# Score masks copied by VectorE, token sums and tail in halves: a recurrent memory-attention step on one core

## The chip, the cores and the metric

The kernel runs on one core of a Trainium2 chip. The metric is the device time of one execution in microseconds (us). Five engines of the core work side by side, each on its own list of instructions: TensorE (PE in the profile, its weight loads PEld), VectorE (DVE), ScalarE (ACT), GpSimd (POOL) and SyncE (SP, which issues DMAs). PE writes its results into eight banks of the accumulator memory PSUM, which DVE and ACT read and write too.

## The reference

The output mixes two branches per token with a gate. Branch B is a two-layer MLP over all 2048 tokens. Branch A goes through the tokens in 64 segments of 32 and carries a memory of 8 rows from one segment to the next:

```python
g = _sigmoid((x * gate_w).sum(-1, keepdims=True))
idx = jnp.arange(L)                                   # L = 8 + 32
mask = (idx[:, None] < M) | (idx[:, None] >= idx[None, :])
mem = mem0
for s in range(n_seg):                                # 64 segments
    xs = x[:, s * seg_len:(s + 1) * seg_len, :]
    h = jnp.concatenate([mem, xs], axis=1)
    q, k, v = h @ Wq, h @ Wk, h @ Wv                  # 32 heads of 128
    scores = jnp.where(mask, q @ k.T * scale, -1e9)
    o = (softmax(scores) @ v) @ Wo
    mem = o[:, :M]                                    # the next step's memory
    outs.append(o[:, M:])
return g * concat(outs) + (1 - g) * B(x)
```

(The lines are shortened.) A step needs the memory rows that the step before has made.

## The kernel before, in words

First all weights are loaded and branch B is computed, with the product (1 - g) * b stored for later. Then come the 64 steps, and a tail. The order of every instruction on every engine is the order of the code: the part from the MLP to the end stands under `tc.manual_schedule()`, and waits are put in where one engine's result is used by another.

**Rows of a step.** Four segments make one tile T of 128 tokens; a step is `s`, with `T, si = divmod(s, 4)`. The step's input `hT` has 32 columns: 24 of the segment's tokens and the 8 memory rows. The other 8 tokens of each of the four segments do not need the memory for their q, k and v; they are projected a tile ahead, for all four segments together. This work, and the output projection of those left tokens a tile later, is the *side work* (`side`, `left_qk`, `left_v`, `wo_left`): a generator per step of 8 units of four matmuls of 512 columns. `run(n)` issues n of them at the place where it stands. `WS` gives for each `si` the numbers W1, W2 and W3 that `run` gets at three places of the step. The last tile has no next one to project, so its first two steps have no side work.

**One step** on PE, in order:

- q and k of the 32 columns, in four groups of 16 matmuls (`qk_unit`, line 120), for two halves of the heads into banks U0 to U3. Each is cast by ACT to `Tb` (line 125) and turned by a DVE transpose into `QT` or `KT` (line 129).
- `scores(s, 0)`: the scores of heads 0 to 15 into bank SbF, 16 matmuls of line 257 and four of line 261. Before them the mask stands in the bank already, and the scores are added to it. One ACT instruction takes the exponential into `E` (line 706).
- four `v_unit`s of the first value half (line 139) into X1.
- `mask_mm(1)` (line 249): four matmuls of 224 columns that put the mask `Mk`, times the identity, into bank W.
- one unit of the second value half into X2, then `msum(0)` (lines 268 and 271): the exponentials' sums for the 8 memory queries, which DVE turns into reciprocals (line 702) and multiplies into E (line 703). These two are `mnorm`.
- `scores(s, 1)` into bank W, and two exponentials of it (line 695), the memory queries' first.
- two more units of the second value half, `msum(1)` and `mnorm(1)`, the last unit. ACT casts the two value halves to `V` (lines 710 and 724).
- W1 units of side work; `xsums` (line 614): 16 matmuls of four columns, the sums for the token queries, into 8 columns of bank SbF. `recip_x` takes their reciprocals on DVE (line 625), sends them through DRAM to all partitions (`Rb`), copies the memory reciprocals (line 631) and adds them to `racc` on POOL. The token rows are normalised with `Rb` only in the next step, on POOL (line 640).
- `av` (lines 281 and 286): probabilities times values, first heads 0 to 15, then 16 to 31, into U0 to U3. ACT casts the memory rows to `UT` (line 732), then the token rows to `XR`.
- W2 units; the output projection `wo_pass` (line 151), 32 matmuls into bank W, cast in two halves to `w` (line 647).
- `mask_mm(0)` for the next step into SbF; W3 units; for the first step of a tile `out_sel`, which puts a finished tile's output together; then `new_mem` (line 654), which turns the 8 memory rows of w into columns. DVE casts them into the next step's `hT` (line 656), on which the next q and k wait.

**Last step and tail.** Step 63 needs no new memory. The sums of its tokens go into SbF (`sums`), DVE takes a reciprocal of 256 columns (line 760) and multiplies it into E, while PE runs `out_sel` for the last tile but one and the projection of step 62. Then come `av`, `wo_left` (eight units), the projection of step 63, and the last tile's output: five selecting matmuls into X2 (lines 786 and 788), one DVE instruction (line 791) and one DMA. Beside it runs a check: DVE reduces `rmin` and `racc` (lines 777 and 778) to `good`, one matmul (line 783) counts the good partitions, and a branch that is not taken here would repeat the branch in a safe form.

Of the kernel before, what the change touches and what calls it, by code (L numbers as in the profile page):

```python
# [27 lines left out]
def kernel(ctx, tc, A_x, A_mem0, A_Wq, A_Wk, A_Wv, A_Wo, A_seg_len, B_x, B_w1, B_b1, B_w2, B_b2, gate_w, out):  # L28
# [46 lines left out]
    Mk = ep.tile([P, 4, EW], BF16)  # L75
# [171 lines left out]
    def mask_mm(i2):  # L247
        for j in range(4):
            nc.tensor.matmul(Sb[i2][32 * j:32 * j + 32], lhsT=ident[:, 32 * j:32 * j + 32], rhs=Mk[:],  # L249
                             start=True, stop=True, skip_group_check=True, tile_position=(0, 32 * j))  # L250
# [41 lines left out]
    with tc.tile_pool(name="mlpw", bufs=1) as mlpw, \  # L292
# [70 lines left out]
        nc.gpsimd.memset(Mk[:], 0.0)  # L363
# [212 lines left out]
    mask_mm(0)  # L576
# [29 lines left out]
    xs8 = SbF[:, 256:256 + NG]  # L606
    RW = 9 * NG

    def xsums(s, E):

        for first, c0, n in ((True, 8, 32), (False, 0, LEFT)):
            for i in range(NG):
                c, h = i % 4, i // 4
                nc.tensor.matmul(xs8[32 * c:32 * c + n, 4 * h:4 * h + 4], lhsT=E[:, i, c0:c0 + n], rhs=BO[:, 0:P:32],  # L614
                                 start=first and h == 0, stop=not first, skip_group_check=True, tile_position=(0, 32 * c))
# [7 lines left out]
    def recip_x(s):  # L623
        R = Rs.pop(s)
        nc.vector.reciprocal(out=R[:, 8 * NG:RW], in_=xs8)

        Rb = cw.tile([P, P, NG], FP32, tag="Rb", bufs=1, name="Rb")
        nc.sync.dma_start(r_dr[s % 2][:], R[:, 8 * NG:RW])
        nc.sync.dma_start(Rb[:].rearrange("p r e -> p (r e)"), r_dr[s % 2][:].rearrange("r e -> (r e)").partition_broadcast(P))
        for i2 in (1, 0):  # L630
            nc.vector.tensor_copy(out=R[:, 32 * i2:32 * i2 + 32], in_=RP[i2])
        nc.gpsimd.tensor_tensor(out=racc[:, 0:RW], in0=racc[:, 0:RW], in1=R[:, 0:RW], op=ALU.add)  # L632
        Rbs[s] = Rb
# [25 lines left out]
    WS = ((3, 2, 0), (2, 2, 2), (2, 2, 2), (2, 2, 2))  # L659
    for s in range(nseg):  # L660
# [18 lines left out]
        for n, (t, hf) in enumerate(((0, 0), (1, 0), (0, 1), (1, 1))):  # L679
# [6 lines left out]
            qk_tr(qk_cast(bk[:]), (QT, KT)[t], hf, LEFT * (1 - t))  # L686
        V = cw.tile([P, NG, Dh], BF16, tag="V", name="V")
# [21 lines left out]
        mask_mm(1)  # L709
        nc.scalar.copy(out=v_out(V, 0), in_=X1[:])  # L710
        v_unit(X2, hc, 1, 0)
        if not last:
            msum(0)
            mnorm(0)
# [3 lines left out]
        for kc in range(1, 3):  # L718
            v_unit(X2, hc, 1, kc)
        if not last:  # L720
            msum(1)
            mnorm(1)
        v_unit(X2, hc, 1, 3)
        nc.scalar.copy(out=v_out(V, 1), in_=X2[:])  # L724
        if last:
            break
        run(W1)
        xsums(s, E)
# [10 lines left out]
        mask_mm(0)  # L739
# [17 lines left out]
    for _ in out_sel(T - 1, X2):  # L757
        pass
    nc.gpsimd.memset(UL[T % 2][:, :, :, LEFT * si:seg], 0.0)
# [10 lines left out]
    for _ in wo_left(T, X1):  # L770
# [3 lines left out]
    nc.gpsimd.tensor_tensor(out=racc[:, nx], in0=racc[:, nx], in1=R[:, nx], op=ALU.add)  # L774
# [7 lines left out]
    wf = wo_pass(UF)  # L782
    nc.tensor.matmul(X1[0:1, 0:1], lhsT=good[:, 0:1], rhs=good[:, 1:2], start=True, stop=True)
    bad = okp.tile([1, 1], I32)
    nc.vector.tensor_scalar(out=bad[:], in0=X1[0:1, 0:1], scalar1=-1.0, scalar2=float(P), op0=ALU.mult, op1=ALU.add)
    nc.tensor.matmul(X2[:], lhsT=SelL[:], rhs=wls.pop(T)[:], start=True, stop=False, skip_group_check=True)
    for i in range(SPT):
        nc.tensor.matmul(X2[32 * i:32 * i + 32, :], lhsT=(SelR if i < si else SelI)[:], rhs=(ws.pop(SPT * T + i) if i < si else wf)[:],
                         start=False, stop=True, skip_group_check=True, tile_position=(0, 32 * i))
    o = cw.tile([P, Dm], BF16, tag="o", name="o")  # L790
    nc.vector.scalar_tensor_tensor(out=o[:], in0=X2[:], scalar=g_all[:, T:T + 1], in1=cs.pop(T)[:], op0=ALU.mult, op1=ALU.add)
    nc.sync.dma_start(out2[T * P:(T + 1) * P, :], o[:])
# [123 lines left out]
```

## Time and profile before

| | us |
|---|---|
| median of 3 runs | 777.28 |
| runs | 776.89 to 779.0 |
| profiled execution | 779.11 |
| its span, first to last instruction | 777.3 |
| granted TensorE clock, share | 0.997 |
| MLP and loads (until the first step) | 0 to 95.97 |
| steps 0 to 62 | 95.97 to 757.14 |
| step 63 and tail | 757.14 to 777.3 |

How its rows are read. A row of the groups has line, engine, operation, output<-inputs, shape, count, then busy time in us, mean ns of one instruction, and the engine's idle time before them with what ended it. A row of the timeline has start in us, length, engine, line, operation, output<-inputs, count of merged instructions, and in brackets the idle time before it and the releaser. A row of the chain has start, length in the chain, engine, output and line, count. A row of the table by stretches has the stretch, its length, and for PE, PEld, DVE, ACT and POOL the busy time and the number of instructions in it, then the clock and the DMA share and rate. Matmuls on different 32-column parts of the array overlap, so a group's mean length is not what one of them costs.

### The profile page before, as it was taken

The numbers are of one execution on the slowest core, as the hardware profiler recorded it, in microseconds if no ns is written. First come the engines' busy times: TensorE is split into PE (matmuls) and PEld (weight loads), VectorE is DVE, ScalarE is ACT, GpSimd is POOL, SyncE is SP. The second block draws the span as 40 slices with busy tenths as digits, with TensorE's granted clock in tenths as the row PEclk, the third lists the DMA queues.
The fourth block names the chain that finished last, engine by engine and source line by source line (L and its number), as shares of the span: only waits on it lengthen the run. The fifth ranks groups of instructions, "written<-read, shape, count | busy, mean of one in ns | idle before, by whom it ended". The sixth has DMA issues, their size and how long they took to land.

```text
span 777.3 us, 44300 instructions
## 1 busy us (share of the span) xinstructions
PE 759.5 (98%) x19673; PEld 419.6 (54%) x19687; DVE 345.4 (44%) x1235; ACT 529.6 (68%) x1439; POOL 278.6 (36%) x523
## 2 busy tenths in 40 slices
PE   7999999999999999999999999999999999999996
PEld 5666555555555555555555555555555555555453
DVE  5776344434334343434444444435343434444334
ACT  4666676677767677667777777677776777676663
POOL 4111034333344433344434333443334344343342
PEclk9999999999999999999999999999999999999999
DMA  6779421222121222212132312212222212122221
GB/s 194 276 248 387 137 58 62 75 61 90 62 71 54 77 72 74 77 57 74 51 88 61 89 62 79 67 56 72 78 72 65 83 36 88 61 81 62 70 61 44
DMA packets 53174, 70.61 MB, mean 91 GB/s; under 512 B 21289, under 2 KB 42898, under 8 KB 51442
## 3 DMA queue, kind: packets, MB, share of 16 engines
q1 hardware_dynamic: 51250, 64.84, 26.4%
q8 instruction: 156, 2.56, 1.4%
q0 software_dynamic: 784, 1.97, 0.7%
q10 hardware_dynamic: 944, 0.92, 0.4%
q14 instruction: 40, 0.33, 0.1%
HBM read 56.96 MB, written 4.45 MB: 79 GB/s over the span
## 4 chain that ended last, share of the span: by engine, by line
PE 96%; DVE 2%; issue 1%; DMA 1%; ACT 0%; POOL 0%; DVEq 0%; ACTq 0%; POOLq 0%
PE U L120 29%; PE X L139 18%; PE W L151 15%; PE X L120 7%; PE U L466 4%; PE X L151 4%; PE U L281 3%; PE SbF L460 2%; PE W L460 2%; PE U L654 2%; PE U L268 1%; PE W L257 1%; PE SbF L257 1%; PE W L249 1%; PE SbF L614 1%
## 5 line engine op out<-in xcount | busy, mean ns | idle before, releaser
L640 POOL TENSOR_TENSOR UT<-XR,Rb 128x384 bf16<-128x384 bf16 x126 | 140.2, 1134 | 305.8 <-DMA Rb<-r_dr 226.2
L125 ACT CAST Tb<-U 128x512 bf16<-128x512 f32 x258 | 151.0, 585 | 76.4 <-PE U L120 75.9
L120 PEld LDWEIGHTS <-hT 128*32 128x32 bf16 x4096 | 104.5, 96 | 109.4 <-DVE hT L656 16.2
L139 PE MATMUL X<-Wv_sb,hT 128*32 128x512 bf16 x2048 | 151.4, 379 | 0.0
L120 PE MATMUL U<-Wq_sb,hT 128*32 128x512 bf16 x2048 | 133.3, 380 | 0.5 <-DVE hT L656 0.2
L120 PE MATMUL U<-Wk_sb,hT 128*32 128x512 bf16 x2048 | 132.6, 379 | 0.0
L151 PE MATMUL W<-Wo_sb,UT 128*32 128x512 bf16 x2080 | 125.7, 380 | 1.9 <-ACT UT L732 1.2
L656 DVE CAST hT<-U 128x16 bf16<-128x16 f32 x126 | 21.9, 175 | 207.6 <-PE U L654 199.9
L129 DVE STREAM_TRANSPOSE QT<-Tb 128x256 f32<-128x256 f32 x128 | 57.0, 446 | 80.3 <-ACT Tb L125 80.2
L151 PEld LDWEIGHTS <-UT 128*32 128x32 bf16 x2080 | 58.6, 96 | 57.7 <-issue 17.4
L620 ACT CAST XR<-U 128x256 bf16<-128x256 f32 x252 | 78.6, 439 | 0.0
L129 DVE STREAM_TRANSPOSE KT<-Tb 128x256 f32<-128x256 f32 x128 | 57.0, 446 | 46.8 <-ACT Tb L125 46.8
L647 ACT CAST w<-W 128x256 bf16<-128x256 f32 (+1 forms) x128 | 41.9, 378 | 49.0 <-PE W L151 49.0
L640 POOL TENSOR_TENSOR UL<-XR,Rb 128x128 bf16<-128x128 bf16 x126 | 60.2, 500 | 0.0
L139 PEld LDWEIGHTS <-hT 128*32 128x32 bf16 x2048 | 49.0, 94 | 20.7 <-issue 0.2
L632 POOL TENSOR_TENSOR racc<-racc,R 128x72 f32<-128x72 f32 x63 | 21.2, 337 | 99.1 <-PE U L286 69.9
L732 ACT CAST UT<-U 128x64 bf16<-128x64 f32 x252 | 35.3, 227 | 28.2 <-PE U L286 28.2
L724 ACT CAST V<-X 128x512 bf16<-128x512 f32 x64 | 37.4, 585 | 22.5 <-PE X L139 22.5
L466 PE MATMUL U<-w_sb,hTm 128*128 128x512 bf16 (+1 forms) x163 | 49.5, 381 | 0.6
L460 PEld LDWEIGHTS <-w_sb 128*128 128x128 bf16 (+1 forms) x352 | 34.6, 102 | 19.5 <-issue 1.3
L710 ACT CAST V<-X 128x512 bf16<-128x512 f32 x64 | 37.5, 585 | 9.4 <-PE X L139 1.1
L125 ACT CAST Tb<-X 128x512 bf16<-128x512 f32 x62 | 36.9, 595 | 8.0 <-PE X L120 6.2
(158 smaller groups left out, 1169.9 us busy)
## 6 DMA issues: line engine op xcount, KB each, us to landing
Rb<-r_dr SPq DMA_DIRECT2D x63, 512.0 KB, 4.0
Wv_sb<-in_A_Wv_dram SPq DMA_DIRECT2D x4, 1024.0 KB, 6.4
Wq_sb<-in_A_Wq_dram SPq DMA_DIRECT2D x4, 1024.0 KB, 7.1
Wk_sb<-in_A_Wk_dram SPq DMA_DIRECT2D x4, 1024.0 KB, 9.6
Wo_sb<-in_A_Wo_dram SPq DMA_DIRECT2D x4, 1024.0 KB, 15.3
VP<-VL SPq DMA_DIRECT2D x64, 64.0 KB, 3.3
c<-c_dr SPq DMA_DIRECT2D x16, 128.0 KB, 2.9
out_dram<-o SPq DMA_DIRECT2D x16, 128.0 KB, 1.9
```

Source lines behind the costliest of these rows:

```text
L120: nc.tensor.matmul(bk[32 * j:32 * j + 32, :], lhsT=G[:, kc, :], rhs=W5[t][:, kc, h0:h1, j, :], start=(kc == 0), stop=(kc == KC - 1), tile_ ...
L125: nc.scalar.copy(out=Tb[:], in_=bk.rearrange("p (a b e) -> p a e b", a=8, b=2))
L129: nc.vector.transpose(out=dst[:, 8 * hf:8 * hf + 8, c0:c0 + 32, :].rearrange("p a r b -> p a (r b)").bitcast(FP32), in_=Tb[:].rearrange("p ...
L139: nc.tensor.matmul(bk[32 * j:32 * j + 32, :], lhsT=G[:, kc, :], rhs=Wv5[:, kc, 4 * vb:4 * vb + 4, j, :], start=(kc == 0), stop=(kc == KC - ...
L151: nc.tensor.matmul(bk[32 * c:32 * c + 32, :], lhsT=U_[:, j, i, :], rhs=Wo_sb[:, 4 * i + j, :], start=(n == 0), stop=(n == NW - 1), tile_po ...
L460: nc.tensor.matmul(hp[:rows, 0:TB * P], lhsT=w1_sb[:, kc, fc * P:fc * P + rows], rhs=yTs[blk][:, kc, :], start=(kc == 0), stop=(kc == KC - 1))
L466: nc.tensor.matmul(bp(blk, tt)[:], lhsT=hTm[blk % 2][:rows, fc, tt * P:(tt + 1) * P], rhs=w2_sb[:rows, fc, :], start=(fc == 0), stop=(fc = ...
L620: nc.scalar.copy(out=XR[:, j], in_=U[j][:, 0:NG * 40].rearrange("p (i q) -> p i q", q=40)[:, :, 0:32])
L640: nc.gpsimd.tensor_tensor(out=out[:, :, 4 * h:4 * h + 4, o:o + b - a], in0=XR[:, :, 4 * h:4 * h + 4, a:b], in1=Rb[:, h, :, :, a:b], op=ALU ...
L647: nc.scalar.copy(out=w[:, a:a + Dm // parts], in_=W[:, a:a + Dm // parts])
L710: nc.scalar.copy(out=v_out(V, 0), in_=X1[:])
L724: nc.scalar.copy(out=v_out(V, 1), in_=X2[:])
```

## The change

- The mask is no longer made by PE. `mask_put(i2)` is one DVE copy from `MkF` into the bank. For bank W it stands after the first transpose of the step; for bank SbF it stands at the end of `recip_x`, for the next step, and covers 8 further columns with zeros, where the token sums are then added.
- `xsums` is cut in two: the eight matmuls of heads 0 to 15 stand ahead of `msum(0)`, the other eight where all stood.
- `msum(1)` and `mnorm(1)` stand behind the last value unit, and not ahead of it. The cast of the second value half is issued ahead of them in the code.
- `WS` moves one unit of side work from ahead of the projection to behind it, in the steps with si of 1, 2 and 3.
- Tail: `out_sel` writes bank X1; three of the eight `wo_left` units stand ahead of step 62's projection; racc's last sum goes from POOL to DVE; the last projection is cast in halves; the selecting matmuls that do not need it stand ahead of the check's matmul and write two banks by halves of the columns; the last matmul, the DVE instruction and the output DMA come in two halves each.

```diff
-    Mk = ep.tile([P, 4, EW], BF16)
+    MkF = ep.tile([P, 4 * EW + NG], BF16)
+    Mk = MkF[:, 0:4 * EW].rearrange("p (a c) -> p a c", c=EW)
...
-    def mask_mm(i2):
-        for j in range(4):
-            nc.tensor.matmul(Sb[i2][32 * j:32 * j + 32], lhsT=ident[:, 32 * j:32 * j + 32], rhs=Mk[:],
-                             start=True, stop=True, skip_group_check=True, tile_position=(0, 32 * j))
+    def mask_put(i2):
+        c = 4 * EW + (NG if i2 == 0 else 0)
+        nc.vector.tensor_copy(out=(SbF, W)[i2][:, 0:c], in_=MkF[:, 0:c])
...
-    xs8 = SbF[:, 256:256 + NG]
+    xs8 = SbF[:, 4 * EW:4 * EW + NG]
...
-    def xsums(s, E):
-
-        for first, c0, n in ((True, 8, 32), (False, 0, LEFT)):
-            for i in range(NG):
-                c, h = i % 4, i // 4
-                nc.tensor.matmul(xs8[32 * c:32 * c + n, 4 * h:4 * h + 4], lhsT=E[:, i, c0:c0 + n], rhs=BO[:, 0:P:32],
-                                 start=first and h == 0, stop=not first, skip_group_check=True, tile_position=(0, 32 * c))
+    def xsums(E, h):
+
+        for c0, n in ((8, 32), (0, LEFT)):
+            for c in range(4):
+                nc.tensor.matmul(xs8[32 * c:32 * c + n, 4 * h:4 * h + 4], lhsT=E[:, 4 * h + c, c0:c0 + n], rhs=BO[:, 0:P:32],
+                                 start=False, stop=True, skip_group_check=True, tile_position=(0, 32 * c))
...
             nc.vector.tensor_copy(out=R[:, 32 * i2:32 * i2 + 32], in_=RP[i2])
+        mask_put(0)
...
-    WS = ((3, 2, 0), (2, 2, 2), (2, 2, 2), (2, 2, 2))
+    WS = ((3, 2, 0), (2, 1, 3), (2, 1, 3), (2, 1, 3))
...
             qk_tr(qk_cast(bk[:]), (QT, KT)[t], hf, LEFT * (1 - t))
+            if n == 0:
+                mask_put(1)
...
-        mask_mm(1)
         nc.scalar.copy(out=v_out(V, 0), in_=X1[:])
         v_unit(X2, hc, 1, 0)
         if not last:
+            xsums(E, 0)
             msum(0)
             mnorm(0)
...
-        for kc in range(1, 3):
+        for kc in range(1, KC):
             v_unit(X2, hc, 1, kc)
-        if not last:
-            msum(1)
-            mnorm(1)
-        v_unit(X2, hc, 1, 3)
         nc.scalar.copy(out=v_out(V, 1), in_=X2[:])
         if last:
             break
+        msum(1)
+        mnorm(1)
         run(W1)
-        xsums(s, E)
+        xsums(E, 1)
...
-        mask_mm(0)
         run(W3)
...
-    for _ in out_sel(T - 1, X2):
+    nc.gpsimd.memset(UL[T % 2][:, :, :, LEFT * si:seg], 0.0)
+    for _ in out_sel(T - 1, X1):
         pass
-    nc.gpsimd.memset(UL[T % 2][:, :, :, LEFT * si:seg], 0.0)
+    fill = wo_left(T, X2)
+    run(3)
...
-    for _ in wo_left(T, X1):
+    for _ in fill:
         pass
...
-    nc.gpsimd.tensor_tensor(out=racc[:, nx], in0=racc[:, nx], in1=R[:, nx], op=ALU.add)
+    nc.vector.tensor_tensor(out=racc[:, nx], in0=racc[:, nx], in1=R[:, nx], op=ALU.add)
...
-    wf = wo_pass(UF)
-    nc.tensor.matmul(X1[0:1, 0:1], lhsT=good[:, 0:1], rhs=good[:, 1:2], start=True, stop=True)
+    wf = wo_pass(UF, 2)
+
+    wl, c = wls.pop(T), cs.pop(T)
+    halves = ((X1, slice(0, Dm // 2)), (X2, slice(Dm // 2, Dm)))
+    for bk, cc in halves:
+        for i in range(SPT):
+            nc.tensor.matmul(bk[32 * i:32 * i + 32, cc], lhsT=SelL[:, 32 * i:32 * i + 32], rhs=wl[:, cc], start=True, stop=False,
+                             skip_group_check=True, tile_position=(0, 32 * i))
+        for i in range(si):
+            nc.tensor.matmul(bk[32 * i:32 * i + 32, cc], lhsT=SelR[:], rhs=ws[SPT * T + i][:, cc], start=False, stop=True,
+                             skip_group_check=True, tile_position=(0, 32 * i))
+    nc.tensor.matmul(U[0][0:1, 0:1], lhsT=good[:, 0:1], rhs=good[:, 1:2], start=True, stop=True)
...
-    nc.vector.scalar_tensor_tensor(out=o[:], in0=X2[:], scalar=g_all[:, T:T + 1], in1=cs.pop(T)[:], op0=ALU.mult, op1=ALU.add)
-    nc.sync.dma_start(out2[T * P:(T + 1) * P, :], o[:])
+    for bk, cc in halves:
+        nc.tensor.matmul(bk[32 * si:32 * si + 32, cc], lhsT=SelI[:], rhs=wf[:, cc], start=False, stop=True,
+                         skip_group_check=True, tile_position=(0, 32 * si))
+        nc.vector.scalar_tensor_tensor(out=o[:, cc], in0=bk[:, cc], scalar=g_all[:, T:T + 1], in1=c[:, cc], op0=ALU.mult, op1=ALU.add)
+        nc.sync.dma_start(out2[T * P:(T + 1) * P, cc], o[:, cc])
```

10 lines of the change are left out of this document (3 added, 7 removed).

## The prediction

> **What bounds the kernel now.** I read the page's engine totals first, then the groups of the lines that go, the chain that ended last, a table of single memory steps, and the timeline inside three of them.
>
> ```profile
> span 777.3 us, 44300 instructions
> PE 759.5 (98%) x19673; PEld 419.6 (54%) x19687; DVE 345.4 (44%) x1235; ACT 529.6 (68%) x1439; POOL 278.6 (36%) x523
> ```
> ```profile
> L249 PE MATMUL SbF<-Mk,ident 128*32 128x224 bf16 x256 | 19.2, 259 | 0.0
> L249 PE MATMUL W<-Mk,ident 128*32 128x224 bf16 x256 | 17.5, 259 | 0.0
> ```
> ```profile
> 405.46 0.10 PE W L249 x4
> ...
> 407.22 0.10 PE SbF L614 x15
> ...
> 410.11 0.10 PE SbF L249 x4
> ```
>
> Matmuls overlap, so the chain's shares count: each group of four mask matmuls holds 0.10 us of it, two per step. On this reading PE is the bound and the 128 groups are worth 12.8 us. The table of single steps says otherwise: a first step of a tile, a later step with side work, and a step of the last tile, which has no side work.
>
> ```profile
> 348.50:359.17 10.67, 10.67 (x308) 5.76 (x308) 3.94 (x16) 7.70 (x22) 4.05 (x7) 1.00 0.26 63
> 411.16:421.49 10.33, 10.33 (x300) 5.54 (x297) 4.82 (x17) 7.21 (x21) 4.07 (x7) 1.00 0.14 40
> 736.47:746.80 10.33, 9.24 (x264) 4.94 (x264) 4.38 (x15) 6.49 (x19) 4.02 (x7) 1.00 0.27 78
> ```
>
> The third has 36 matmuls fewer and PE idle for 1.09 us, and lasts as long as the second. So 48 of the 63 steps (10.33 us) are set by the round trip from the memory rows back to themselves; only the 15 first steps of tiles (10.67 us) have PE work on it. In the step without side work the waits name the round trip's links:
>
> ```profile
> 742.50 0.58 ACT L724 CAST V<-X 128x512 bf16<-128x512 f32 x1 [0.35 <-PE X L139]
> 743.14 0.17 PEld L281 LDWEIGHTS <-V 32*128 32x128 bf16 x16 [0.17 <-ACT V L724]
> 743.86 1.91 PE L151 MATMUL W<-Wo_sb,UT 128*32 128x512 bf16 x32 [0.41 <-ACT UT L732]
> 746.24 0.49 PE L654 MATMUL U<-SelM,w 128*32 128x8 bf16 x16 [0.38 <-ACT w L647]
> ```
>
> The second half of av waits for the second value cast, the projection for UT, the new memory for w. From the step's start these stand at 6.67, 7.39 and 9.77 us. The step with side work has them at the same places:
>
> ```profile
> 415.46 0.45 DVE L129 STREAM_TRANSPOSE KT<-Tb 128x256 f32<-128x256 f32 x1 [0.37 <-ACT Tb L125]
> 415.96 0.18 PEld L257 LDWEIGHTS <-KT 128*32 128x32 bf16 x16
> 416.12 0.63 PE L139 MATMUL X<-Wv_sb,hT 128*32 128x512 bf16 x8
> 416.41 0.42 ACT L695 ACTIVATE E<-W 128x64 bf16<-128x64 f32 x2
> 416.68 0.20 PE L268 MATMUL U<-E,BO 128*32 128x32 bf16 x4
> 417.03 0.37 DVE L702 RECIPROCAL W<-U 128x32 f32<-128x32 f32 x1
> 417.18 0.58 ACT L724 CAST V<-X 128x512 bf16<-128x512 f32 x1 [0.35 <-PE X L139]
> 417.44 0.22 DVE L703 TENSOR_TENSOR E<-E,W 128x64 bf16<-128x64 bf16 x1
> 417.82 0.27 PE L281 MATMUL U<-E,V 32*128 32x40 bf16 x16
> 418.54 1.91 PE L151 MATMUL W<-Wo_sb,UT 128*32 128x512 bf16 x32
> 420.92 0.21 PE L654 MATMUL U<-SelM,w 128*32 128x8 bf16 x8
> ```
>
> (Its start is 411.16: 6.66, 7.38, 9.76.) The Trainium skill, "Perfetto Trace Analysis", section "Identifying the Most-Contended Engine", says that matmul busy time is no good measure, and to take weight-load busy time. By that, 98% is not the bound and 54% leaves room; the equal steps agree.
>
> **The change, part by part.**
>
> *Mask for bank W.* Four matmuls (0.10 us) leave the place ahead of the second scores, and eight token-sum matmuls come in, half of line 614's 0.10: PE arrives 0.05 us earlier. But KT is transposed by 415.46 + 0.45 = 415.91 and its load begins 0.05 later, at 415.96. That stays. Worth 0.
>
> *The second memory sums* move behind the last value unit. Today they start at 416.68, just after the first exponential (416.41 + 0.21, half of the row's 0.42, + 0.06). Three units at 0.21 from 416.12 end at 416.76: 0.08 later. From the sums to the reciprocal is 0.35 and to the end of line 703 another 0.63, so E is ready at 417.74 and av's second half goes on 0.05 later, at 417.79, against 417.82. The value cast is no longer last: its last unit starts at 416.55 (416.12 and two units), no longer behind the sums of 416.68 with their 0.05 of issue, so the cast's 417.18 + 0.58 = 417.76 becomes 417.57. What is late next is therefore the DVE pair. Gain 0.03 us in each of 48 steps, 1.4 us; the ends are 0.19 (were the cast alone to set it, at 417.63) and -0.1 (the sums 0.13 later than I reckon). I take 0.03, since every link of the DVE pair is read from the row of the same instruction. Queued behind the waiting av are the rest of av, UT, the projection and the next step.
>
> *The same in the first steps*, with three side units between sums and av:
>
> ```profile
> 354.02 0.20 PE L268 MATMUL U<-E,BO 128*32 128x32 bf16 x4
> ...
> 354.94 0.27 PE L614 MATMUL SbF<-BO,E 128*32 128x4 bf16 x16
> ...
> 355.28 0.28 PE L281 MATMUL U<-E,V 32*128 32x40 bf16 x16
> ```
>
> Here 1.26 us of PE work runs from sums to second av. A value unit (0.21) and half the token sums (0.05) leave it: 1.00. Started 0.08 later, av's second half comes at 355.10; by the DVE pair (354.10 + 0.35 + 0.63 + 0.05) at 355.13. Gain 0.15 us in 15 steps, 2.2 us.
>
> *Mask for bank SbF and the side units (WS).* Its 0.10 us and two units lay between projection and new memory, where even an empty PE waits for w (746.24, above). One unit comes over from ahead of the projection: 1.71 + 0.64 = 2.35 us, inside the 2.38 from 418.54 to 420.92. Ahead of the projection the empty PE waits for UT as well, so the unit's departure gives nothing. Worth 0 and 0; cover gone, 0.1 per step.
>
> *The copies on DVE*, 128 of 224 or 232 columns. No row shows a copy into PSUM. Nearest rows:
>
> ```profile
> L768 DVE CAST UT<-U 128x256 bf16<-128x256 f32 x2 | 0.8, 420 | 0.6 <-PE U L286 0.6
> ...
> L791 DVE SCALAR_TENSOR_TENSOR o<-X,g_all,c 128x512 bf16<-128x512 f32 x1 | 0.8, 751 | 0.9 <-PE X L788 0.9
> ```
> ```profile
> 413.74 0.45 DVE L129 STREAM_TRANSPOSE KT<-Tb 128x256 f32<-128x256 f32 x1 [0.36 <-ACT Tb L125]
> ...
> 414.62 0.27 PE L257 MATMUL SbF<-QT,KT 128*32 128x40 bf16 x16
> ```
>
> I take 0.40, from the cast of like width; the far end is 0.75. W's copy falls into the 0.36 us ahead of the first KT transpose, whose result, at 414.19, the first scores need at 414.62 less the 0.05 of a wake-up and a load of 0.02: 0.36 + 0.36 = 0.72 us of cover. What stands behind it on DVE is that transpose. SbF's copy follows line 631 near 418.2, and DVE's next work on the round trip is the hT cast after 420.92. Worth 0 at either end, 51 us more DVE time.
>
> *The tail.* Three of eight leftover units move ahead of the last projection, into the time of DVE's long reciprocal.
>
> ```profile
> 768.58 0.42 DVE L773 TENSOR_TENSOR rmin<-rmin,R 128x256 f32<-128x256 f32 x1
> 768.76 1.90 PE L151 MATMUL W<-Wo_sb,UT 128*32 128x512 bf16 x32
> 769.95 0.16 DVE L781 TENSOR_SCALAR good<-tot 128x1 bf16<-128x1 f32 x1
> 770.71 0.58 ACT L647 CAST w<-W 128x512 bf16<-128x512 f32 x1 [1.14 <-PE W L151]
> 771.34 0.38 PE L788 MATMUL X<-w,SelI 128*32 128x512 bf16 x1
> 771.76 0.75 DVE L791 SCALAR_TENSOR_TENSOR o<-X,g_all,c 128x512 bf16<-128x512 f32 x1 [0.87 <-PE X L788]
> ```
>
> The projection starts 0.64 earlier, at 768.12, and its casts in halves end near 770.5 and 770.75. The check loses ground: racc's add joins DVE's queue (0.41, as rmin's), so `good` is ready at 770.52 instead of 770.11, and its matmul now stands ahead of the two last ones, which then start at 770.64 and 770.79: 0.55 before 771.34. DVE's two halves of 0.4 end at about 771.8, for 772.51. SP issues two DMAs instead of one, the second by about 772.2, for 772.5. I take PE's 0.55; the ends are 0 (the check holds the tail) and 0.75.
>
> *Sum:* 1.4 + 2.2 + 0.55 = 4.2 us. The profiled execution took 779.11 us (span 777.3 and 1.8 around it), which the change would take to 774.9. It is 1.8 above the median of 777.28; the same 4.2 off the median gives 773.1.
>
> **The rivals.**
>
> *PE is the bound after all:* 12.8 + 0.55 us go, 763.9. For it: 98% busy. Against it: the equal steps with and without side work. Chance 0.04.
>
> *Only the ends move:* the DVE pair turns out as late as the cast was, or 0.05 later; the first steps keep 0.1 and the tail 0 to 0.5. 15 x 0.1 + 0.25 - 48 x 0.01 = 1.3 us, 776.0. For it: my margin is 0.03 us, and it rests on reading 0.02 us off the timeline. Chance 0.22.
>
> *Slower: the second sums arrive late.* If DVE can start its reciprocal only when the value unit ahead has run its whole recorded 0.40 us, and not its 0.21 of streaming, then E is ready 0.19 us later still: av at 417.98, 0.16 us lost in 48 steps and 0.04 in 15, 8.3 us less the tail's 0.55, 785.0. It decides from 0.10 us above my reckoning on (63 x 0.10 against 4.2, plus 2.3). Against it: today's second sums, at 416.68, also follow value units closely, and their 0.35 us to the reciprocal holds. Chance 0.08.
>
> *The pauses move.* PE sometimes stops with nothing to wait for:
>
> ```profile
> 502.51 0.09 PEld L151 LDWEIGHTS <-UL 128*32 128x32 bf16 x1 [1.01 <-issue]
> ```
> ```profile
> 95.97:757.14 661.17, 655.28 (x18668) 351.97 (x18662) 278.66 (x986) 466.06 (x1303) 257.83 (x456) 1.00 0.23 69
> ```
>
> The 63 steps take 661.17 us; 15 x 10.67 + 48 x 10.33 is 655.9, so such pauses hold 5.3 us. In the instruction order the long ones stand 256 PE instructions, or a multiple of it, apart, and bite just behind the dense av matmuls. The change shortens a step by 16 PE instructions, so they fall elsewhere. Between none and double that is -5.3 to +5.3 us; I expect about as many. To turn 4.2 us into a loss above 2.3 it would take more than double: 0.03. The Trainium skill, "Runtime: NRT & Kernel Launch", section "Instruction fetch mechanics", tells of blocks of 256 instructions whose fetch is mostly hidden; the spacing agrees, the hiding not everywhere.
>
> **How the numbers follow.** A measurement of this kernel can tell about 0.3%, 2.3 us, from no change. The forecast's own case has 0.63 and, with pauses varying by some 2 us, lies at 770.5 to 775.5. Faster: 0.04, most of the forecast (0.60) and a quarter of the second rival (0.06) make 0.70. Slower: 0.08 + 0.03 = 0.11. Same: 0.19. For 8 in 10 the range leaves out the PE-bound case and the slow one and takes in the second rival with its pauses: 770.0 to 778.0.
>
> **What would show it.** Right: later steps still near 10.30 us, first steps near 10.52; the second av waiting for line 707's E (DVE) where it waited for V; the second scores still 0.05 us behind the KT transpose; no idle time of the scores on either copy; the last matmul about 0.5 us nearer to the end of the last av. Wrong: later steps at 10.1 us (PE-bound) or above 10.4 (late sums), a copy above 0.7 us, or PE pauses that sum to over 8 us.

## The result, and the profile after

The changed kernel took 774.57 us (median of 11, 772.65 to 776.31), the kernel before 777.39 beside it (median of 11, 776.62 to 779.0): a ratio of 0.9961, with a 95% interval of 0.9949 to 0.9972. The forecast was 773.1, with a range of 770.0 to 778.0. The time fell inside and on the side foretold, but by the medians the change saved 2.8 us where the sum had 4.2. One term of the sum (the order of the second sums in later steps) brought nothing, another (the masks), set at nothing, was worth something by itself, and in the profiled execution part of the gain came from fewer pauses of PE, which the forecast had not counted on.

The page's first rows, changed kernel:

```profile
span 773.6 us, 43533 instructions
PE 752.6 (97%) x19186; PEld 416.9 (54%) x19186; DVE 385.6 (50%) x1365; ACT 528.1 (68%) x1440; POOL 278.4 (36%) x522
```

PE lost 6.9 us of busy time and DVE gained 40. The profiled execution took 775.35 us, 3.76 less than the profiled one of before; its span is 3.7 less. The table of stretches of the changed kernel (length, then busy time and instructions of PE, PEld, DVE, ACT, POOL, then clock, DMA share, GB/s) has all 63 steps, a first step of a tile, and a later step with side work:

```profile
97.68:753.86 656.18, 646.42 (x18163) 348.63 (x18162) 318.76 (x1113) 464.62 (x1303) 258.66 (x456) 1.00 0.23 69
...
388.76:399.28 10.52, 10.48 (x300) 5.65 (x300) 4.63 (x18) 7.67 (x22) 4.07 (x7) 1.00 0.33 97
409.65:419.99 10.34, 10.27 (x293) 5.53 (x289) 5.42 (x19) 7.17 (x21) 4.04 (x7) 1.00 0.10 28
```

Against the rows of before: a later step takes 10.34 us and took 10.33; a first step takes 10.52 and took 10.67. The 63 steps together lost 661.17 - 656.18 = 5.0 us. Their regular part, 48 x 10.34 + 15 x 10.52 = 654.1, is 1.8 below the 655.9 of before. The other 3.2 are nearly all pauses: what single steps take beyond the usual length of their kind sums to 2.2 us, and summed to 5.3. (Each kernel has one profiled execution, so each such sum is that of one execution.) Ahead of the steps the changed kernel stood 1.7 us worse (97.68 for 95.97). Of the changed work only the first mask for bank SbF lies there. The kernels of the experiments below, without added work there, start their steps at 95.6 to 97.4 whichever of the two ways that mask is made, so I count it as scatter. From step 63 to the end it is 773.6 - 753.86 = 19.74 for 20.16.

The timeline inside the later step that starts at 409.65:

```profile
414.45 0.28 PE L259 MATMUL W<-QT,KT 128*32 128x40 bf16 x16
...
414.87 0.42 ACT L699 ACTIVATE E<-W 128x64 bf16<-128x64 f32 x2
...
415.25 0.19 PE L270 MATMUL U<-E,BO 128*32 128x32 bf16 x4
...
415.47 0.59 ACT L724 CAST V<-X 128x512 bf16<-128x512 f32 x1 [0.19 <-PE U L273]
...
415.63 0.37 DVE L706 RECIPROCAL W<-U 128x32 f32<-128x32 f32 x1 [0.28 <-PE U L273]
...
416.04 0.22 DVE L707 TENSOR_TENSOR E<-E,W 128x64 bf16<-128x64 bf16 x1
...
416.31 0.28 PE L283 MATMUL U<-E,V 32*128 32x40 bf16 x16
```

What the second half of av waits for has changed. The value cast ends at 415.47 + 0.59 = 416.06, 6.41 us into the step (before: 417.76, 6.60). The DVE pair ends at 416.26, 6.61 into the step (before: 417.66, 6.50). The second half of av goes on at 416.31, 6.66 into the step, where it was. This table puts these and the later kernels' marks side by side (us from the start of a later step, from the timelines; "end of E" is the end of line 707's product, 703 in the kernel before):

| kernel | second scores start | second exponentials start | second sums start | reciprocal starts | end of E | end of value cast | second half of av | later step | first step |
|---|---|---|---|---|---|---|---|---|---|
| before | 4.82 | 5.25 | 5.53 | 5.88 | 6.50 | 6.61 | 6.66 | 10.33 | 10.67 |
| changed | 4.81 | 5.22 | 5.60 | 5.98 | 6.61 | 6.41 | 6.66 | 10.34 | 10.52 |
| masks by DVE alone | 4.81 | 5.20 | 5.47 | 5.82 | 6.44 | 6.55 | 6.61 | 10.28 | 10.62 |
| order of sums alone | 4.82 | 5.25 | 5.61 | 6.00 | 6.62 | 6.43 | 6.68 | 10.35 | 10.56 |
| masks, token halves | 4.81 | 5.22 | 5.50 | 5.85 | 6.47 | 6.58 | 6.64 | 10.31 | 10.60 |
| masks, order | 4.81 | 5.20 | 5.60 | 5.98 | 6.61 | 6.41 | 6.66 | 10.33 | 10.52 |
| changed, last unit split | 4.81 | 5.22 | 5.50 | 5.85 | 6.47 | 6.47 | 6.53 | 10.21 | 10.40 |

(Medians over the steps 8 to 59. The first steps of the split kernel, about half of which hold a pause, are given as the undisturbed ones take.) The copies, by the groups of lines:

```profile
L252 DVE CAST SbF<-MkF 128x232 f32<-128x232 bf16 x64 | 25.8, 403 | 2.2
L252 DVE CAST W<-MkF 128x224 f32<-128x224 bf16 x64 | 23.4, 366 | 0.0
```

0.40 and 0.37 us, as taken; the first scores start 3.46 us into the step as before, so neither copy is seen on the path.

The end of the kernel, whose step 63 starts at 753.86 (before: 757.14):

```profile
764.36 1.90 PE L153 MATMUL W<-Wo_sb,UT 128*32 128x512 bf16 x32
...
766.40 0.16 DVE L784 TENSOR_SCALAR good<-tot 128x1 bf16<-128x1 f32 x1
...
766.73 0.54 PE L801 MATMUL X<-w,SelI 128*32 128x256 bf16 x2
...
767.44 0.47 DVE L803 SCALAR_TENSOR_TENSOR o<-X,g_all,c 128x256 bf16<-128x256 f32 x1
```

The projection starts 10.50 into step 63 (11.62 before), the last DVE instruction ends at 14.05 (15.37 before). Of these 1.3 us only 0.42 reach the end of the span: behind DVE's last instruction the kernel of before ran on for 777.3 - 772.51 = 4.8 us, this one for 773.6 - 767.91 = 5.7.

### The profile page after: what moved, and what is told of

Same layout as the page of the kernel before. It is cut to its first block, busy times and chain, and to the rows that moved or that the text cites. A ratio compares the mean times of both kernels' runs of the same rounds, so it can differ in the third digit from the quotient of the medians.

```text
span 773.6 us, 43533 instructions
## 1 busy us (share of the span) xinstructions
PE 752.6 (97%) x19186; PEld 416.9 (54%) x19186; DVE 385.6 (50%) x1365; ACT 528.1 (68%) x1440; POOL 278.4 (36%) x522
## 4 chain that ended last, share of the span: by engine, by line
PE 94%; POOL 2%; DVE 1%; DMA 1%; issue 1%; ACT 1%; DVEq 0%; ACTq 0%; POOLq 0%
PE U L122 29%; PE X L141 17%; PE W L153 16%; PE X L122 7%; PE U L468 5%; PE U L283 5%; PE X L153 3%; PE SbF L462 2%; PE W L462 2%; POOL racc L634 2%; PE W L259 1%; PE U L656 1%; PE U L288 1%; PE SbF L259 1%; DMA b1r<-in_B_b_dram 1%; PE SbF L615 1%
## 5 line engine op out<-in xcount | busy, mean ns | idle before, releaser
L122 PEld LDWEIGHTS <-hT 128*32 128x32 bf16 x4096 | 104.6, 96 | 109.7 <-DVE hT L658 15.7
L141 PE MATMUL X<-Wv_sb,hT 128*32 128x512 bf16 x2048 | 132.7, 378 | 0.0
L153 PEld LDWEIGHTS <-UT 128*32 128x32 bf16 x2080 | 56.9, 96 | 58.6 <-issue 19.0
L141 PEld LDWEIGHTS <-hT 128*32 128x32 bf16 x2048 | 45.8, 95 | 26.7
L468 PE MATMUL U<-w_sb,hTm 128*128 128x512 bf16 (+1 forms) x176 | 53.0, 385 | 0.0
L283 PE MATMUL U<-E,V 32*128 32x40 bf16 x2048 | 42.5, 178 | 1.7 <-DVE W L706 1.3
```

Source lines behind the costliest of these rows:

```text
L122: nc.tensor.matmul(bk[32 * j:32 * j + 32, :], lhsT=G[:, kc, :], rhs=W5[t][:, kc, h0:h1, j, :], start=(kc == 0), stop=(kc == KC - 1), tile_ ...
L141: nc.tensor.matmul(bk[32 * j:32 * j + 32, :], lhsT=G[:, kc, :], rhs=Wv5[:, kc, 4 * vb:4 * vb + 4, j, :], start=(kc == 0), stop=(kc == KC - ...
L153: nc.tensor.matmul(bk[32 * c:32 * c + 32, :], lhsT=U_[:, j, i, :], rhs=Wo_sb[:, 4 * i + j, :], start=(n == 0), stop=(n == NW - 1), tile_po ...
L283: nc.tensor.matmul(Uv[j][:, i, :], lhsT=V[q, i, :], rhs=E[q, i, 8:48], start=(i == 0), stop=False, skip_group_check=True, tile_position=(3 ...
L468: nc.tensor.matmul(bp(blk, tt)[:], lhsT=hTm[blk % 2][:rows, fc, tt * P:(tt + 1) * P], rhs=w2_sb[:rows, fc, :], start=(fc == 0), stop=(fc = ...
```

## The experiments

My theory at the start was that the steps are bound by a round trip and that the masks stood in PE's waiting time; the first rival was that PE's work itself is the bound. The first four experiments take the change apart and try a cure for the new wait. Ratios are against the kernel before on the same chip: 777.86 us for these four; 777.45 for the two that add one part to the masks, the split with late token sums and the shift by 64 matmuls; 777.68 for the other three.

### Masks by DVE alone

```diff
 (kernel before)
-    def mask_mm(i2): ...four matmuls with ident...
+    def mask_put(i2):
+        c = 4 * EW + (NG if i2 == 0 else 0)
+        nc.vector.tensor_copy(out=(SbF, W)[i2][:, 0:c], in_=MkF[:, 0:c])
```

with the copies at the places of the change, and both halves of the token sums at the old late place.

> Kernel before with only the masks put by the DVE copies: eight mask matmuls (0.20 us of PE in 10.33) leave each step, all else stays where it was. My theory (the steps are bound by round trips, the masks stand in PE's waiting time): later steps 10.33 and first steps 10.67 us as before, time within 0.2% of the kernel before (776 to 779 us); no score matmul waits for a copy. Rival (PE is the bound): every step loses 0.20 us, 12.8 us in all, 764.5. Rival (the copies cost DVE time on the path): steps longer by 0.05 or more, 780 or above.

Measured: 773.56 us (median of 6), ratio 0.9945, interval 0.9932 to 0.9958. None of the three theories: every step, first and later, is 0.05 us shorter (10.279 for 10.333 in later steps). 63 x 0.053 = 3.3 us, and the pauses sum to 2.9 us instead of 5.3. This part of the change alone is no slower than the whole change (their intervals overlap). Timeline of its step that starts at 408.61:

```profile
413.41 0.28 PE L257 MATMUL W<-QT,KT 128*32 128x40 bf16 x16
...
413.80 0.42 ACT L697 ACTIVATE E<-W 128x64 bf16<-128x64 f32 x2
...
414.07 0.20 PE L268 MATMUL U<-E,BO 128*32 128x32 bf16 x4
...
414.57 0.59 ACT L725 CAST V<-X 128x512 bf16<-128x512 f32 x1 [0.35 <-PE X L140]
...
415.21 0.27 PE L281 MATMUL U<-E,V 32*128 32x40 bf16 x16
```

The second scores start where they did, 4.80 into the step, pinned by KT as I had read. But the exponentials that wait for them start 0.39 later and not 0.43 (415.98 to 416.41 in the kernel before). From there on everything, sums, last value unit, cast and av, is 0.05 to 0.06 earlier. So the mask matmuls ahead of the scores were on the path: the first score matmul is issued on time behind the KT transpose, and what follows it still stood in a queue behind masks and memory sums. That the queue in PE is the cause is a reading; that taking 0.10 us of PE work out ahead of the scores moves the exponentials by 0.055 at an unmoved start of the scores is what the run shows. (The run also takes SbF's mask out. That one stands behind the projection; the 0.05 is gained before it, as av shows, and the new memory is earlier by no more than that (9.705 us into the step for 9.759), so it adds nothing.)

### The order of the second sums alone

```diff
 (kernel before)
-        for kc in range(1, 3):
+        for kc in range(1, KC):
             v_unit(X2, hc, 1, kc)
-        if not last:
-            msum(1)
-            mnorm(1)
-        v_unit(X2, hc, 1, 3)
         nc.scalar.copy(out=v_out(V, 1), in_=X2[:])
         if last:
             break
+        msum(1)
+        mnorm(1)
```

> Kernel before with only the second memory sums and their reciprocal moved behind the last value unit; masks by PE, token sums whole at the old place, old tail. My theory after the result (the sums need 0.38 us to the reciprocal, not 0.35, so the DVE pair takes the place of the value cast at the same time): later steps 10.33 to 10.35, first steps 10.55 (0.12 shorter), 1.8 us less in all, 775.5 give or take 1.5 for pauses. Prediction's figure: later steps 10.30, 3.2 us less, 774.1. Rival (late sums): later steps 10.40 or more, 780 or above.

Measured: 776.94 us (median of 12), ratio 0.9989, interval 0.9980 to 0.9998: at the upper edge of the theory's 774 to 777. The steps are as it had them, later ones 10.35, first ones 10.56. The sums start at 5.61 into the step, as the prediction reckoned (5.60), but the reciprocal follows 0.39 behind them and not 0.35, and the pair ends at 6.62, past the 6.61 at which the cast used to end. By the steps that is 48 x 0.013 lost and 15 x 0.116 won, 1.1 us in all; the medians show 0.9.

### The tail alone

```diff
 (kernel before)
+    fill = wo_left(T, X2)
+    run(3)
 ...
-    nc.gpsimd.tensor_tensor(out=racc[:, nx], in0=racc[:, nx], in1=R[:, nx], op=ALU.add)
+    nc.vector.tensor_tensor(out=racc[:, nx], in0=racc[:, nx], in1=R[:, nx], op=ALU.add)
 ...
-    wf = wo_pass(UF)
+    wf = wo_pass(UF, 2)
 ... (last projection, output and its DMA in two halves, as in the change)
```

> Kernel before with only the tail of the change (leftover units ahead of the projection, racc's add on DVE, the last projection in halves). My theory: the 63 steps are as before but for pauses; from the start of step 63 to the end 0.4 to 0.6 us less than 20.16, so 776.5 to 777.2 by the median. The E times R product of the tail takes 0.22 us instead of 0.75, since POOL's add no longer runs beside it. Rival (the end is held by SP's second DMA and PE's last branch, whatever PE's work does): 20.16 stays, no change.

Measured: 777.96 us (median of 11), ratio 0.9997, interval 0.9986 to 1.0007: by the times nothing can be told, and the 0.7 to 1.4 us that were expected off the median are not there. The profiles tell a little. From step 63 to the end it is 19.76 us. Over the five profiles with the old tail (before, and four experiments) this stretch is 19.83 to 20.22, mean 20.06; over the eight with the new one (in one of them with the addition on POOL) 19.41 to 19.76, mean 19.60. By these the tail is worth 0.46 us. The product of E and R takes 0.22 us, as expected. The last DVE instruction ends 14.37 us into step 63 here and at 14.96 to 15.03 in the four other experiments with the old tail: 0.6 earlier, as reckoned.

### The last value unit split around the sums

```diff
 (changed kernel)
-        for kc in range(1, KC):
-            v_unit(X2, hc, 1, kc)
+        for kc in range(1, 3):
+            v_unit(X2, hc, 1, kc, True)
+        v_half(X2, hc, 1, 3, 0)        # columns 0:256
+        if not last:
+            msum(1)
+            mnorm(1)
+        v_half(X2, hc, 1, 3, 1)        # columns 256:512
 ...
-    WS = ((3, 2, 0), ...
+    WS = ((2, 2, 1), ...
```

> Changed kernel with the last value unit cut into two column halves, the second memory sums between them, and the side units of first steps placed 2, 2, 1. My theory: av's second half is bound by two nearly equal chains, the value cast (6.41 after the step's start) and the reciprocal and product on DVE (6.605); with the sums half a unit earlier both end at about 6.50, av's second half starts at 6.56 instead of 6.66, every later step takes 10.24 to 10.26 and every first step 10.42 to 10.45: 5 to 6 us less than the changed kernel, 768.5 to 770. Rival (what sets the step is PE's amount of work, or another chain such as the first half of av): steps 10.30 or more, 773 to 775. Rival (four more instructions of half width and their loads cost PE as much as they win): 10.33, 774.

Measured: 768.52 us (median of 4), ratio 0.9879, interval 0.9865 to 0.9894. The theory held, with more gain in a step than it gave (10.21 for 10.24 to 10.26, first steps 10.40 for 10.42 to 10.45). Its step that starts at 407.35:

```profile
412.57 0.42 ACT L704 ACTIVATE E<-W 128x64 bf16<-128x64 f32 x2
...
412.85 0.20 PE L275 MATMUL U<-E,BO 128*32 128x32 bf16 x4
...
413.21 0.36 DVE L711 RECIPROCAL W<-U 128x32 f32<-128x32 f32 x1
...
413.24 0.58 ACT L734 CAST V<-X 128x512 bf16<-128x512 f32 x1 [0.25 <-PE X L146]
...
413.61 0.22 DVE L712 TENSOR_TENSOR E<-E,W 128x64 bf16<-128x64 bf16 x1
...
413.88 0.28 PE L288 MATMUL U<-E,V 32*128 32x40 bf16 x16
```

Pair and cast end within 0.01 us of each other (413.83 and 413.82), 0.13 ahead of where the pair of the changed kernel ended, and the step is 0.13 shorter. This answers the PE-bound rival too: with the same columns in four more matmuls, the step falls by 0.13. The regular part loses 48 x 0.13 + 15 x 0.12 = 8.0 us against the changed kernel; pauses of 4.7 us instead of 2.2 give 2.5 of it back. That leaves 5.5, where the 63 steps of the two profiles differ by 656.18 - 650.79 = 5.4 and the medians by 6.0. In first steps the side units moved too, so their 0.12 is not the split's alone.

### Which part spends what the masks win

Two kernels add one part each to the masks alone.

```diff
 (masks alone)                      masks and token halves:
         if not last:
+            xsums(E, 0)
             msum(0)
 ...
         run(W1)
-        xsums(E, 0)
         xsums(E, 1)
```

> Masks by DVE (as in the first experiment) and the token sums in halves, the first half ahead of the first memory sums; second memory sums and tail as before. My theory now: whatever PE does ahead of the second scores counts, although they start behind the KT transpose, because they are still queued behind it when they start. The eight token sums put there give back about half of what the masks won: the second exponentials on ACT end at 5.45 after the step's start (masks alone 5.42, kernel before 5.48), later steps 10.30 to 10.31 (masks alone 10.28, before 10.33), first steps 10.56 to 10.60 (10.62, 10.67). Time by the steps 48 x 0.025 + 15 x 0.09 = 2.5 us less than before, 775.3 at equal pauses. Rival (the first token sums stand in waiting time, as the prediction had it): the exponentials still end at 5.42 and later steps take 10.28.

Measured: 773.92 us (median of 8), ratio 0.9958, interval 0.9943 to 0.9973; exponentials from 5.22 to 5.45, later steps 10.31, first steps 10.60. The eight token-sum matmuls ahead of the memory sums cost the later steps half of what the masks had won. (The time went 3.5 us down and not 2.5. In the profiled execution the pauses are 2.9 us and not 5.3, more than the difference.)

The other has the diff of the order, put on top of the masks alone:

> Masks by DVE and the second memory sums behind the last value unit; token sums whole at the old late place, old tail. My theory: the exponentials end at 5.42, the sums start at 5.53 to 5.55, the DVE pair ends at 6.55 to 6.57 where the value cast ended with masks alone (6.55), so later steps stay at 10.28 to 10.30 and first steps drop to 10.48 to 10.52: 48 x 0.04 + 15 x 0.17 = 4.5 us less than before, 773.4 at equal pauses, 1 to 3 us below the whole change. Rival (the order's loss is larger than the masks' gain, as in the whole change): later steps 10.33.

Measured: 774.69 us (median of 6), ratio 0.9963, interval 0.9949 to 0.9977; later steps 10.33, first steps 10.52. Here my theory fell and the rival held. Its step that starts at 410.07:

```profile
415.27 0.42 ACT L697 ACTIVATE E<-W 128x64 bf16<-128x64 f32 x2
...
415.67 0.19 PE L268 MATMUL U<-E,BO 128*32 128x32 bf16 x4
...
416.06 0.37 DVE L704 RECIPROCAL W<-U 128x32 f32<-128x32 f32 x1 [0.34 <-PE U L271]
...
416.46 0.22 DVE L705 TENSOR_TENSOR E<-E,W 128x64 bf16<-128x64 bf16 x1
...
416.73 0.28 PE L281 MATMUL U<-E,V 32*128 32x40 bf16 x16
```

The exponentials are 0.03 us earlier than in the changed kernel, and it makes no difference: the sums now wait for three value units, which start behind the second scores whatever the exponentials do. So with the sums behind the last unit little of the masks' gain reaches av: against the order alone its second half goes on 0.02 earlier (6.66 for 6.68), where the masks alone bring 0.05. The order costs a later step 0.05 us against the masks alone and wins a first step 0.10: 48 x 0.05 - 15 x 0.10 = 0.9 us lost.

### The split with the token sums late

```diff
 (last unit split)
         if not last:
-            xsums(E, 0)
             msum(0)
 ...
         run(W1)
+        xsums(E, 0)
         xsums(E, 1)
```

> The split last value unit with the token sums whole at the old late place. My theory: the second exponentials end 0.03 earlier (5.42 for 5.45), and with them the sums between the halves, the DVE pair (6.44) and the value cast (6.44): later steps 10.18, first steps 10.38 to 10.42, 1.5 to 2 us less than the split with early token sums (768.52), 766.5 to 767. Rival (the eight token sums that come back ahead of av delay it, or the exponentials are not what holds the pair): later steps 10.21 or more, 768.5 or more.

Measured: 768.98 us (median of 6), ratio 0.9890, interval 0.9870 to 0.9910. The rival held: the exponentials do end 0.03 earlier (5.42), but the sums start at 5.49 for 5.50 and steps are 10.21. The half unit ahead of them, not E, sets the sums' start.

### Side units of first steps

```diff
 (last unit split)
-    WS = ((2, 2, 1), ...
+    WS = ((3, 2, 1), ...
```

> The split last value unit (token sums in halves, as in the first run of the split), with one side unit more ahead of av in first steps (3, 2, 1), so that one fewer stands between the last new memory and the next step's first projection. In the first steps of the split kernel two units there (0.42 us) held the next step's start 0.20 behind the hT cast. My theory: av's second half of first steps comes 0.03 to 0.06 later, the step's end 0.21 earlier; first steps 10.25 to 10.30 instead of 10.42, later steps 10.21 as they were, 15 x 0.15 = 2.2 us less than 768.5, 766.3 at equal pauses. Rival (first steps are held by their PE work wherever it stands): 10.42, 768.5.

Measured: 768.20 us (median of 4), ratio 0.9882, interval 0.9866 to 0.9899. First steps take 10.31 for 10.40, later ones 10.22: most of the theory, though 0.01 above its range. The 63 steps take 649.51 us for 650.79, with about the same pauses. The 766.3 foretold is not there, and by the times the two kernels can't be told apart. Both beat the changed kernel by 6 us.

### Do the pauses belong to places in the program?

```diff
 (changed kernel, ahead of the first step)
+        for _ in range(64):        # 128 in the second kernel
+            nc.tensor.matmul(U[3][:, 0:1], lhsT=ident[:], rhs=ident[:, 0:1], start=True, stop=True, skip_group_check=True)
```

> Changed kernel with 64 matmuls of one column (128 PE instructions with their loads) added ahead of the first step, which do nothing for the result. Theory (the pauses belong to the place of an instruction in PE's program, one block of 256 after another): the pauses of the changed kernel in steps 3, 36, 40, 44 and 51 go, and others appear where the 256-instruction border now falls just behind the dense av matmuls; their sum may be anything from 0.5 to 5 us. Rival (the pauses come from DMA traffic or the side work of those steps): they stay in the same steps, 2.2 us in all.

> Changed kernel with 128 matmuls of one column (256 PE instructions with their loads) ahead of the first step. Theory (the pauses belong to blocks of 256 instructions counted through PE's whole program): a shift by one whole block leaves them where the changed kernel had them, in steps 36, 40, 44 and 51 beside the 0.37 us of step 3, and in none of the steps of the shift by 128 (4, 8, 12, 16, 27); sum 1.5 to 3 us, time within 0.2% of the changed kernel. Rival (any change of the start reshuffles them): other steps.

Measured: 774.50 us (median of 7) and 775.17 (median of 5), ratios 0.9961 (0.9949 to 0.9974) and 0.9964 (0.9949 to 0.9978). Rows of PE's weight loads in which a pause ends, with its length in brackets; changed kernel (steps 36 and 40), shift by 128 (12, 16, 27), shift by 256 (36, 40, 44):

```profile
479.57 0.10 PEld L122 LDWEIGHTS <-GL 128*32 128x32 bf16 x4 [0.71 <-issue]
...
521.48 0.10 PEld L283 LDWEIGHTS <-V 32*128 32x128 bf16 x2 [0.54 <-issue]
```
```profile
229.19 0.12 PEld L122 LDWEIGHTS <-GL 128*32 128x32 bf16 x8 [0.42 <-issue]
...
270.97 0.11 PEld L283 LDWEIGHTS <-V 32*128 32x128 bf16 x6 [0.38 <-issue]
...
382.33 0.34 PEld L141 LDWEIGHTS <-hT 128*32 128x32 bf16 x12 [0.18 <-issue]
```
```profile
479.99 0.10 PEld L122 LDWEIGHTS <-GL 128*32 128x32 bf16 x4 [1.09 <-issue]
...
521.60 0.10 PEld L283 LDWEIGHTS <-V 32*128 32x128 bf16 x2 [0.25 <-issue]
...
563.71 0.14 PEld L283 LDWEIGHTS <-V 32*128 32x128 bf16 x12 [0.59 <-issue]
```

The shift by half a block took the pauses of steps 36, 40, 44 and 51 away and put others into steps 4, 8, 12, 16, 27 and 52, 2.3 us in all. The shift by a whole block brought those of 36, 40 and 44 back; that of 51 did not come, and 14 and 55 got one, with smaller ones in 2, 4 and 32 (3.2 us in all). So the rival, DMA traffic or the side work of those steps, falls: neither was changed. Counted in program order, with a weight load and its matmul as two, the longer ones end at the 194th to 196th PE instruction of a block of 256, in all three kernels. So one fixed place in a block is where a pause can stand. Whether it bites there, and how long, differs even between two executions of one PE program. The kernel of the last experiment below has the changed kernel's PE program. Both pause in steps 36, 40 and 44 (0.73, 0.59 and 0.17 us there, 0.44, 0.42 and 0.46 here), but only the one in step 51 and only the other in step 10. That the fetch of instructions is the cause is not shown by these runs.

The 0.37 us of step 3 moves with none of these shifts, and its rows show why: it is VectorE that starts late. In the changed kernel (first row) it is the second reciprocal, 0.76 us behind its sums where 0.38 is usual; in the kernel before it is the cast of the new memory.

```profile
135.25 0.37 DVE L706 RECIPROCAL W<-U 128x32 f32<-128x32 f32 x1 [0.64 <-PE SbF L615]
```
```profile
137.70 0.28 DVE L656 CAST hT<-U 128x16 bf16<-128x16 f32 x2 [3.45 <-PE U L654]
```

In all thirteen traces it is the 320th instruction that the trace has of VectorE, 0.35 to 0.38 us later in its step than in step 7. So it has its place in VectorE's list, not in PE's; why there is open.

### The tail's addition back on POOL

```diff
 (changed kernel)
-    nc.vector.tensor_tensor(out=racc[:, nx], in0=racc[:, nx], in1=R[:, nx], op=ALU.add)
+    nc.gpsimd.tensor_tensor(out=racc[:, nx], in0=racc[:, nx], in1=R[:, nx], op=ALU.add)
```

> Changed kernel with the tail's racc addition back on POOL. My theory: while POOL reads its two tiles, the small E times R product on DVE takes 0.75 us as in the kernel before, not the 0.22 of the changed kernel, and the end of the kernel moves by less than 0.3 us, since PE's projection ends after it. Rival (the 0.75 came from the old order of the tail, not from POOL): 0.22 us here too.

Measured: one run, 773.2 us. DVE's and POOL's rows of its tail:

```profile
760.43 0.75 DVE L767 TENSOR_TENSOR E<-E,R 128x64 bf16<-128x64 bf16 x1
...
760.13 0.97 POOL L777 TENSOR_TENSOR racc<-racc,R 128x256 f32<-128x256 f32 x1 [2.55 <-DVE R L763]
```

The same product in the changed kernel:

```profile
762.30 0.22 DVE L767 TENSOR_TENSOR E<-E,R 128x64 bf16<-128x64 bf16 x1
```

With the addition on POOL the product takes 0.75 us and ends 0.08 behind POOL's addition (761.18 and 761.10); with the addition on DVE it takes 0.22. From step 63 to the end it is 19.41 us, 0.3 less than the changed kernel's profile and inside the spread of the new tail. The theory held in both points.

## Why the prediction was right, and where it was wrong

**"48 of the 63 steps are set by the round trip"**: right. Taking the mask matmuls out saves 0.05 and not 0.20 us per step, and the split of a value unit shortens the step by 0.13 at an equal amount of PE work. PE as the bound (763.9) is out. What the reading missed is that a little of PE's work does lie on the round trip, the part that is queued ahead of the second scores.

**"Mask for bank W ... Worth 0"**: wrong, and the largest error. I pinned the second scores by the start of their first weight load behind the KT transpose, and that start indeed did not move. But what the path needs is their end, and that moved with the PE work ahead: by 0.055 for the masks' 0.10 and by half of that for the eight token sums. That these wait in PE's queue is the likely reason and not shown. Masks alone are worth 0.05 us in each of 63 steps, 3.3 us. The eight token sums in their place give half of that back (exponentials at 5.22, between 5.25 and 5.20).

**"The second memory sums ... gain 0.03 us"**: wrong in size and sign. Sums at 416.76 in my reckoning are 5.60 into the step, measured 5.60; the cast 6.41, measured 6.41; the product's end 0.63 behind the reciprocal's start, measured 0.63. The failed link is "from the sums to the reciprocal is 0.35": that holds where the sums start just behind E (before, masks alone, token halves, first split), but it is 0.38 to 0.39 where they stand behind a value unit (changed kernel, both kernels with the order). The margin was 0.03, so the pair took over exactly where the cast had been: the condition of the second rival (776.0), which held for the later steps. The slower rival needed 0.10 above my reckoning; it was 0.03 to 0.04. Against the masks alone, the step loses 0.05 us by the order.

So the order brought nothing of the 1.4 us that I had from it: in the changed kernel masks (-0.05), token halves (+0.03) and order (+0.03) come to +0.01 in a later step, 0.5 us lost.

**First steps, "0.15 us in 15 steps, 2.2 us"**: right in size (10.52 for 10.67), and mostly by the part named. The order alone takes 0.11 us off a first step (10.56), and 0.10 with the masks by DVE (10.52 for 10.62). The masks, set at nothing, give the other 0.05.

**WS, SbF's mask, the copies on DVE**: nothing contradicts the zeros. The new memory starts 9.75 us into a later step, 9.76 before. SbF's mask and WS were not taken back by themselves.

**The tail, "I take PE's 0.55"**: close, 0.46 by the mean of the profiles. The details were right (projection 1.12 earlier in the pair of profiles, of which 0.35 was a pause of the kernel before; last DVE end 0.6 earlier in the tail alone), but part is lost behind DVE's last instruction.

**The pauses, "I expect about as many"**: wrong in the mean, inside the bounds given. Sums over the 63 steps: 5.3, 4.5 and 3.6 us in the three kernels with masks on PE; 2.1 to 3.2 in the seven with masks on DVE and whole value units; 4.7, 5.8 and 4.6 in the three with the split. Each holds the 0.3 to 0.4 us of step 3. Their places go with the program's layout in blocks of 256, as said. That the fewer PE instructions of the changed step place them better fits the three sets, by about 1.8 us in the mean and 3.1 in the pair of profiles, but with one execution of each kernel it is not shown, and why a given layout should have more stays open.

Together: -1.8 (steps) - 0.45 (tail) - 1.8 (pauses, mean) = -4.1 us, for -2.8 by the medians and -3.7 by the pair of profiles. The mean of the pauses is the weakest of the three terms. The prediction's 4.2 had 1.4 from a term that turned out slightly negative, and none from the pauses, which stood in for part of it. It was right on the direction and on what bounds the kernel. Its size, half as large again as the medians show, came as near as it did partly by luck.

## What to carry to other kernels

The start of a group of matmuls in the record is not proof that what lies ahead of it is free: read when the first instruction that consumes the group starts, and compare that distance between places where PE had waited and places where it had not. Where two chains end within about 0.1 us of each other, moving a whole unit of work from one to the other can merely swap which is late (here 6.50 and 6.61 became 6.61 and 6.41). Cutting the moved unit so that both end together, at 6.47, won 6 us more, twice what the whole change had won. A change in parts should be run in parts: here its first part alone (773.56) did as well as all of it (774.57).

## What the runs showed of the hardware that I had not expected

A DVE product with two SBUF inputs waits out a POOL addition of two SBUF inputs: 0.75 us beside it, ending 0.08 to 0.09 behind it, and 0.22 without. It was 0.75 or 0.76 in the six traces with this addition on POOL and 0.22 in the seven with it on DVE; the experiment above changes nothing but the engine of the addition. The Trainium skill, "SBUF — State Buffer", section "Who interferes with whom", says that DVE shares a pair of SBUF ports with GpSimd and that the sharing is an exclusive lock; the rows agree.

PE's pauses, spaced by multiples of 256 instructions, are 0.1 to 1.2 us each. With the 0.3 to 0.4 us of VectorE in step 3 they sum to 2.1 to 5.8 us, up to 0.8% of this kernel's time. By the Trainium skill, "Runtime: NRT & Kernel Launch", section "Instruction fetch mechanics", instructions come in blocks of 256 and crossing a border is mostly hidden: the spacing and the shift by 128 and 256 agree, and "mostly" leaves room for what is seen here.

Between DVE's last instruction and the end of the span lie 4.8 us in the kernel before and 5.7 in the changed one, so two thirds of the 1.3 us that the shorter tail won on the engines did not reach the end in this pair of profiles.
